# Attention and two feed-forward layers on one core: constant rows set once per buffer, zero rows and k's second copies moved by transfers, q loaded once for both chunks, h1 tiles stored in pairs

## The chip, the core and the metric

The kernel runs on one core of a Trainium2 chip. The metric is the device time of one execution in microseconds (us); the time before is the median of three runs. The engines are TensorE (PE, its weight loads shown apart as PEld), VectorE (DVE), ScalarE (ACT), GpSimd (POOL) and SyncE (SP), on whose queue almost all transfers (DMAs) are issued.

## What is computed

A decay attention over 4 batches, 8 heads, 576 rows and 64 columns a head, then two feed-forward layers on the 2304 x 512 result:

```python
scores = scale * np.matmul(q, k.transpose(0, 1, 3, 2))
cum = np.cumsum(np.log(np.clip(f, 0.0001, 1.0)), axis=-1)
decay = cum[:, :, :, None] - cum[:, :, None, :]
scores = np.where(causal, -1000000000.0, scores + decay)
attn = np.exp(scores - np.max(scores, axis=-1, keepdims=True))
attn = attn / (np.sum(attn, axis=-1, keepdims=True) + 1e-09)
x = np.matmul(attn, v)                 # then heads side by side: 2304 x 512
h = x @ w_in;   x = (h * (1.0 / (1.0 + np.exp(-1.702 * h)))) @ w_out
h = x @ w_in2;  out = (np.maximum(h, 0.0) + alpha * np.minimum(h, 0.0)) @ w_out2
```

All is fp32; a product is made from a rounded high part and a low remainder of each operand (fp32r), which is why casts and subtractions surround every matmul.

## The kernel before

Every operation is handed to a planner (`Plan.add`) with the engines that may run it, a duration for each, the buffers that it reads and writes, and a priority. `Plan.plan` (line 124) then places the operations one by one, each on the engine and at the time at which it could start, and so sets the order of the instructions on every engine and on SP's queue. At run time each engine works through its own list in order and waits on semaphores. A transfer is planned as 1500 ns, its bytes, and 750 ns (line 176), with 230 ns more (`LAT`) until a reader may start; SP is taken as busy for 610 ns an issue (line 198). Where PE would idle in the plan near the start, `run` (line 228) puts filler matmuls on `ident` (line 490) ahead of the operation.

The work has three parts. **Attention** runs until about 340 us. A unit is a pair of heads of a batch; its 576 query rows are two chunks, rows 0 to 255 and 256 to 575. Units 0 to 7 (batch 0) are `old` and get their transposed k and q from PE. Units 8 to 19 (batches 1 to 3) get them as follows. `load_qk` (line 723) loads a tile `raw` by four transfers, one for 32 partitions each, and DVE transposes it into `tk`. `stack` (line 742) makes two operands out of it for each head (`hh`): `KA` or `QA` (a cast, line 749), and `KB` or `QB`, which hold the low part (a subtraction, line 753) in one half of the partitions and a second copy of the high part in the other (line 756, a copy by ACT, DVE or POOL). `KA` and `QA` have constant rows besides: ones and zeros, set by memsets of `refill` (line 620) whenever a buffer is taken again, up to a limit given by its argument `first`, and in `QA` a row of zeros that is written anew for every chunk (line 806), since the row maxima later land in it (line 982 writes rows 0 to 2). `chunk` (line 895) computes scores for the row maxima (lines 925 and 927), masks them and takes the maxima on DVE (line 952), turns these (line 969) and writes them into `QA`. `chunk2` (line 1051) computes the scores again (line 1081, from `KA`, `KB`, `QA`, `QB`), takes the exponential (line 1097), and multiplies with v (lines 1016 and 1044). Operands are prepared `PRE = 2` steps ahead of the chunk that needs them.

**The first product** (`gemm1`, line 1159, matmuls of line 1180) is background work: once the rows of a block are done, its matmuls fill PE wherever a chunk's next operation is not yet ready. A result tile m (of 16 a block) is evacuated by ACT into `gg`, one of three buffers, and stored to `h1scr` (line 1186). **The rest** (lines 1203, 1424 and 1606) is matmul after matmul with streamed operands.

Of the kernel before, what the change touches and what calls it, by code (L numbers as in the profile page):

```python
# [7 lines left out]
F32 = mybir.dt.float32  # L8
# [77 lines left out]
class Plan:  # L86
# [37 lines left out]
    def plan(self, pen, hold_for, back):  # L124


        free = {}
# [24 lines left out]
        while avail:  # L152
# [42 lines left out]
            if eng == "PE":  # L195
                mode = o.mode
            if eng in QUEUE:
                free[QUEUE[eng]] = t + 610.0
                dma = end - 750.0
            else:  # L200
                free[eng] = end
                if port:
                    free["port"] = end
# [44 lines left out]
def kernel(  # L248
# [143 lines left out]

    ones = att.tile([P, 2, P], F32R, name="ones")
    p_z = sb("att", "Z", 2, [P, 2, P], F32R)
    p_raw = sb("att", "raw", 3, [P, S])
    p_tk = sb("att", "tk", 1, [P, S])

    p_ka = sb("att", "KA", 2, [P, 2, S], F32R)
# [130 lines left out]
    def a_move(n):  # L529
        return [*a_copy(n, HALF), ("POOL", c_pool(n), 0.0, True)]  # L530
# [189 lines left out]

    def load_qk(src, b, h0, w, c0, pri, actq):

        raw, T = Buf(p_raw), Buf(p_tk)
        for o in range(0, P, 32):
            hh, e_ = o // 64, o // 32 % 2
            d_ = DMA(32 * w * 4 * 1.6)
            if actq:
                d_.append(("ACTQ", d_[0][1], 300.0))  # L730
            plan.add(d_, lambda e, hh=hh, e_=e_, o=o: E[e].dma_start(
                raw.ap[o:o + 32, 0:w].rearrange("p (n d) -> p n d", d=32),
                src[b, h0 + hh, c0:c0 + w, 32 * e_:32 * e_ + 32].rearrange("(n p) d -> p n d", p=32),
            ), (), [(raw, o)], pri, QLAG if pri < QPRI else 0.0)
        plan.add([("DVE", 1.25 * w + 85.0)], lambda e: nc.vector.transpose(T.ap[:, :w], raw.ap[:, :w]), [raw], [T], pri)
        return T

    def split(T, w, hi, lo, pri):
# [3 lines left out]
    def stack(T, w, big, other, keys, swap, pri):  # L742

        half = [slice(64 * hh, 64 * hh + 64) for hh in range(2)]
        for hh, r in enumerate(half):
            plan.add(a_copy(w, HALF), lambda e, hh=hh, r=r: copy(e, big.ap[r, hh, :w], T.ap[r, :w]), [T], [(big, ("h", hh, k_)) for k_ in keys], pri)
        for hh, r in enumerate(half):  # L750
            x, y = (half[1 - hh], r) if swap else (r, half[1 - hh])
            rb = [(big, ("h", hh, k_)) for k_ in keys]
            plan.add([("POOL", c_pool(w), 0.0, True), ("DVE", c_half(w), BS, True)], lambda e, hh=hh, r=r, y=y: sub(
                e, other.ap[y, hh, :w], T.ap[r, :w], big.ap[r, hh, :w].bitcast(F32)
            ), [T, *rb], [(other, ("l", hh, k_)) for k_ in keys], pri)
            plan.add(a_move(w), lambda e, hh=hh, r=r, x=x: copy(e, other.ap[x, hh, :w], big.ap[r, hh, :w].bitcast(F32)), rb, [(other, ("h", hh, k_)) for k_ in keys], pri)

    RAW0 = {}

# [37 lines left out]
        plan.add([("ACT", c_act(w, True))], lambda e: copy(e, ov(hi), tv()), [T], [(hi, key)], pri)  # L797
        plan.add([("DVE", c_dve(w))], lambda e: sub(e, ov(lo), tv(), ov(hi).bitcast(F32)), [T, (hi, key)], [(lo, key)], pri)

    def prep_q(u, q0, q1, pri, actq, pet, old):  # L800
        b, h0, m = u["b"], 2 * u["hp"], q1 - q0
        first = u["first"]
        qa, qb = (Buf(p_q0), Buf(p_dq0)) if first else (Buf(p_qa), Buf(p_qb))
        if not old:
            refill(qa, OQ, 3 * m, lambda x: ((x[64:67, 0], 1.0), (x[0:64, 1], 0.0), (x[0:3, 1], 1.0)), pri - 1)
            plan.add([("POOL", 0.95 * m + 60.0)], lambda e: E[e].memset(qa.ap[0:1, 1, :m].bitcast(F32), 0.0), (), [(qa, ("d", 1))], pri)
            stack(load_qk(q, b, h0, m, q0, pri, actq), m, qa, qb, [0], True, pri)
            z = None
            if q0:
                z = Buf(p_z)  # L810
                refill(z, OLD - NP, 4 * P, lambda x: ((x, 0.0), (x[64:66, 0, 0:64], 1.0), (x[0:3, 1, 64:P], 1.0), (x[0:1, 1, 64:P], 0.0)), pri - 1)
                for hh in range(2):
                    r = slice(64 * hh, 64 * hh + 64)
                    plan.add(a_copy(64), lambda e, hh=hh, r=r: copy(
                        e, z.ap[r, hh, 64 * hh:64 * hh + 64], qa.ap[r, hh, m - 64:m].bitcast(F32)
                    ), [(qa, ("h", hh, 0))], [(z, hh)], pri)
            return dict(u, z=z, qa=qa, qb=qb)
# [14 lines left out]
        return dict(u, z=z, fdq=fdq, qa=qa, qb=qb, qh=qh, ql=ql, dq=dq)  # L832

    def prep(b, hp, n, pri, early, actq, plain, pet, old):
# [21 lines left out]
            if not first:  # L856
                rows()
        else:
            refill(ka, OLD, 3 * S, lambda x: ((x[64:67, 0], 1.0), (x[0:64, 1], 0.0), (x[0:3, 1], 1.0)), pri - 1)
# [299 lines left out]
    def gemm1(i, pri, vpri):  # L1159
# [13 lines left out]
        for m in range(NM):  # L1173
# [7 lines left out]

            for c0 in range(0, KT, 2):
                plan.add([("PE", 6 * c_mm(n))], lambda e, ph=ph, w=w, c0=c0: hmm(e, ph, w, c0), [(w, (0, 0)), (w, (0, 1)), xh[c0 // 2], xl[c0 // 2]], [ph], pri)
            g = Buf(p_gg)
            plan.add(a_out(n), lambda e, g=g, ph=ph: copy(e, g.ap[:, :n], ph.ap[:, :n]), [ph], [g], vpri)
            plan.add(DMA(P * n * 4), lambda e, g=g, m=m: nc.sync.dma_start(h1scr[:, m, t0:t0 + n], g.ap[:, :n]), [g], [(b_g1, (i, m))], vpri)

    done = {"i": 0}

# [155 lines left out]
    def operands(no, step):  # L1345
        b, hp, cs_ = seq[no]
        actq, pet, old = 2 <= no < ACTP, no < PET, no < OLD
        kv = prep(b, hp, CH[cs_[-1]][1], A0 + step - PRE, b == 0, actq, no < PLAIN, pet, old)
        return [prep_q(kv, *CH[c_], A0 + step + i - PRE, actq, pet, old) for i, c_ in enumerate(cs_)]

    units = {no: operands(no, no) for no in range(NP)}
    for i, (src, bsrc) in enumerate(((chi, b_ch), (cuml, b_cc))):
# [325 lines left out]
```

## Time and profile before

| what | us |
|---|---|
| median of three runs | 980.39 |
| the three runs | 978.27, 980.39, 980.99 |
| the profiled execution | 978.25 |
| its span | 976.5 |
| PE busy in the span | 958.9 (98%) |
| weight loads busy | 899.6 (92%) |
| DVE, ACT, POOL busy | 755.6, 629.3, 130.7 |

The profiled execution took 1.75 us beside its span, and 2.14 us less than the median. Matmuls are pipelined, so that the next one begins while the last is still shown as busy.

### The profile page before, as it was taken

What the parts mean: (1) busy time and instruction counts of PE and PEld (TensorE: products, weight loads), DVE (VectorE), ACT (ScalarE), POOL (GpSimd) and SP (SyncE); (2) the same over time, 40 slices, a digit from 0 to 9 for tenths busy, and PEclk for the clock granted to TensorE, in tenths of its full rate; (3) what the DMA queues carried; (4) which work ended last, traced back from release to release, by engine and by line L of the source; (5) the groups of instructions that cost most, each with busy time, mean ns of one, the idle gap of its engine ahead of it and who ended that gap; (6) DMA issues with size and microseconds to landing.
All of it is one profiled execution on the core that took longest, in us unless ns stands there. A gap on an engine that the chain in (4) does not pass through costs nothing.

```text
span 976.5 us, 18451 instructions
## 1 busy us (share of the span) xinstructions
PE 958.9 (98%) x6343; PEld 899.6 (92%) x6343; DVE 755.6 (77%) x1635; ACT 629.3 (64%) x1310; POOL 130.7 (13%) x273
## 2 busy tenths in 40 slices
PE   8999999999999999999999999999999999999998
PEld 6788899899999999988888988999999999999998
DVE  4889977788877699946558785788668967887876
ACT  6778986888777558867667795575555743333332
POOL 4236643222222102100000000000000000000000
PEclk9999999999999999999999999999999999999999
DMA  7866634444443136757888685778738495543523
GB/s 140 183 196 182 161 88 119 95 98 93 110 106 75 54 104 226 214 176 256 285 324 277 219 254 188 245 267 297 281 114 308 163 381 197 155 148 109 152 76 99
DMA packets 190015, 176.16 MB, mean 180 GB/s; under 512 B 106480, under 2 KB 164736, under 8 KB 187616
## 3 DMA queue, kind: packets, MB, share of 16 engines
q1 hardware_dynamic: 189904, 174.96, 58.1%
q8 instruction: 50, 0.82, 0.4%
q14 instruction: 45, 0.37, 0.1%
q10 hardware_dynamic: 16, 0.01, 0.0%
HBM read 110.95 MB, written 63.90 MB: 179 GB/s over the span
## 4 chain that ended last, share of the span: by engine, by line
PE 82%; DVE 7%; ACT 4%; DMA 3%; issue 2%; SPq 1%; POOL 1%; DVEq 0%; ACTq 0%; POOLq 0%
PE bk L1203 23%; PE bk L1424 20%; PE bk L1606 19%; PE bk L1180 8%; PE bk L1081 3%; PE bk L1016 2%; PE bk L1044 2%; DVE bk L952 1%; DMA u<-dscr 1%; PE bk L1086 1%; DVE el L524 1%; ACT e L1097 1%; PE bk L927 1%; DMA wraw<-in_moe_w_in_dram 1%; DVE KB L524 1%
## 5 line engine op out<-in xcount | busy, mean ns | idle before, releaser
L1203 PE MATMUL bk<-x,wS 128*128 128x384 f32 x912 | 160.4, 335 | 0.3 <-DVE lx L1229 0.2
L1203 PEld LDWEIGHTS bk<-x,wS 128*128 128x128 f32 x912 | 158.1, 188 | 1.2 <-DVE lx L1229 0.5
L1180 PE MATMUL bk<-xh,w 128*128 128x320 f32 (+2 forms) x640 | 156.6, 309 | 0.0
L1424 PE MATMUL bk<-lh,w 128*128 128x512 f32 (+1 forms) x640 | 146.9, 369 | 0.0
L1424 PEld LDWEIGHTS bk<-lh,w 128*128 128x128 f32 x640 | 112.9, 189 | 19.8
L1180 PEld LDWEIGHTS bk<-xh,w 128*128 128x128 f32 x640 | 111.3, 189 | 2.0 <-issue 1.4
L1180 PE MATMUL bk<-xl,w 128*128 128x320 f32 (+2 forms) x320 | 97.3, 304 | 0.1
L952 DVE CUSTOM_DVE_ANT_0 bk<-bk,mask 128x288 f32<-128x288 f32 (+4 forms) x160 | 74.9, 497 | 19.9 <-PE bk L927 17.1
L524 DVE TENSOR_TENSOR ll<-lx,lh 128x512 fp32r<-128x512 f32 (+1 forms) x80 | 50.9, 637 | 49.2 <-PE bk L1424 34.4
L519 ACT CAST x<-x 128x768 fp32r<-128x768 f32 (+3 forms) x57 | 47.3, 858 | 61.6 <-PE bk L1606 47.5
L1424 PE MATMUL bk<-ll,w 128*128 128x512 f32 (+1 forms) x320 | 81.2, 368 | 0.0
L1097 ACT ACTIVATE e<-bk 128x320 f32<-128x320 f32 (+4 forms) x224 | 63.2, 363 | 19.3 <-PE bk L1081 8.3
L1606 PE MATMUL bk<-wS,x 128*128 128x256 f32 x567 | 70.5, 284 | 0.0
L1606 PEld LDWEIGHTS bk<-wS,x 128*128 128x128 f32 x567 | 69.1, 192 | 0.0
L524 DVE TENSOR_TENSOR x<-x,x 128x768 fp32r<-128x768 f32 (+3 forms) x59 | 57.0, 983 | 15.4 <-ACT x L519 15.0
L1606 PE MATMUL bk<-wS,lh 128*128 128x256 f32 x378 | 68.7, 284 | 0.0
L1424 PEld LDWEIGHTS bk<-ll,w 128*128 128x128 f32 x320 | 57.1, 189 | 9.7
L519 ACT CAST lh<-x 128x768 fp32r<-128x768 f32 (+3 forms) x38 | 31.4, 851 | 53.7 <-PE bk L1606 48.4
L1390 ACT ACTIVATE lx<-lx 128x512 f32<-128x512 f32 (+1 forms) x80 | 46.8, 587 | 29.6 <-DVE ll L524 27.0
L1180 PEld LDWEIGHTS bk<-xl,w 128*128 128x128 f32 x320 | 60.5, 189 | 0.8 <-DVE xl L524 0.3
L1606 PEld LDWEIGHTS bk<-wS,lh 128*128 128x128 f32 x378 | 59.0, 192 | 0.0
L519 ACT COPY lx<-bk 128x384 f32<-128x384 f32 x72 | 34.2, 479 | 33.2 <-PE bk L1203 18.0
(230 smaller groups left out, 2153.8 us busy)
## 6 DMA issues: line engine op xcount, KB each, us to landing
h2scr<-lx SPq DMA_DIRECT2D x96, 192.0 KB
wraw<-in_moe_w_in_dram SPq DMA_DIRECT2D x32, 512.0 KB
wraw<-in_moe_w_out_dram SPq DMA_DIRECT2D x32, 512.0 KB
lx<-h1scr SPq DMA_DIRECT2D x64, 256.0 KB
x<-h2scr SPq DMA_DIRECT2D x32, 512.0 KB
w2scr<-wS SPq DMA_DIRECT2D x5, 1792.0 KB
tscr<-wS SPq DMA_DIRECT2D x4, 1792.0 KB
wS<-tscr SPq DMA_DIRECT2D x4, 1792.0 KB
```

The lines of the kernel that those rows point to most:

```text
L519: nc.scalar.copy(dst, src)
L524: E[e].tensor_tensor(dst, a, b, op=ALU.subtract)
L952: plan.add([("DVE", c_dve(c1 - c0))], lambda e, pm=pm, c0=c0, c1=c1, mk=mk, m0=m0, col=col, f0=f0: nc.vector.tensor_tensor_reduce(pm.ap[:, ...
L1016: nc.tensor.matmul(pb[hh].ap[:, c0:c1], vr.ap[:, t, hh, :], e32.ap[:, hh, e0:e0 + m], start=st, stop=sp, skip_group_check=True,)
L1044: nc.tensor.matmul(pb[hh].ap[:l.shape[1], s0 - q0:n], l, rhs.ap[:w, hh, :m], start=st, stop=sp, skip_group_check=True,)
L1081: nc.tensor.matmul(pss[hh].ap[:w, o_:o_ + m], x.ap[r, hh, a:a + w], y.ap[r, hh, s0 - q0:n], start=i == 0, stop=i == 1, skip_group_check=True)
L1097: plan.add([("ACT", c_act(x1 - x0, True))], lambda e, hh=hh, pss=pss, e32=e32, w=w, x0=x0, x1=x1: nc.scalar.activation(e32.ap[:w, hh, :x1 ...
L1180: nc.tensor.matmul(ph.ap[:, :n], w.ap[:, a, c, :], x[c // 2].ap[:, c % 2, :n], start=(c == 0 and j == 0), stop=(c == KT - 1 and j == 2))
L1203: nc.tensor.matmul(out.ap[:, :XH], wt(a, c), x.ap[:, b, c, :], start=(st and c == 0 and i == 0), stop=(c == 1 and i == 2), skip_group_chec ...
L1390: plan.add([("ACT", c_act(n))], lambda e: nc.scalar.activation(g.ap[:, :n], raw.ap[:, :n], AF.Gelu_apprx_sigmoid), [raw], [g], pri)
L1424: nc.tensor.matmul(py[d].ap[:, :n], w[:, a, d * P:(d + 1) * P], (lo if x else h).ap[:, :n], start=(k == 0 and (a, x) == (0, 0)), stop=(k = ...
L1606: nc.tensor.matmul(py[j].ap[:, t * HF:(t + 1) * HF], x.ap[:, q:q + P], w[:, o, a, :], start=(k == 0 and t == 0 and c == 0), stop=(k == NPA ...
```

## The change

Five things. (1) `refill` is given a smaller `first` for `QA` and `KA`, so that the constant rows are set once for each of the two buffers and no longer for the first six uses. (2) The zero row of `QA` comes from row 3 of the same tile, which stays zero, by a transfer. (3) k's second copies (`KB<-KA`) are transfers too. (4) q is loaded for all 576 rows at once by `load_raw`, and both chunks transpose their part of it; `raw` has two buffers, not three. (5) h1 tiles are evacuated into halves of a tile and stored two at a time; `gg` has two such tiles in place of three single ones. In the planner SP is taken as busy for 540 ns an issue in place of 610, which with the rest redraws the order on every engine.

```diff
-                free[QUEUE[eng]] = t + 610.0
+                free[QUEUE[eng]] = t + 540.0
...
-    p_gg = sb("p1", "gg", 3, [P, BW])
+    p_gg = sb("p1", "gg", 2, [P, 2, BW])
...
-    p_raw = sb("att", "raw", 3, [P, S])
+    p_raw = sb("att", "raw", 2, [P, S])
...
-    def load_qk(src, b, h0, w, c0, pri, actq):
+    def load_raw(src, b, h0, w, c0, pri, actq):
-        raw, T = Buf(p_raw), Buf(p_tk)
+        raw = Buf(p_raw)
...
+        return raw
+    def load_qk(src, b, h0, w, c0, pri, actq, raw=None, r0=0):
+        T = Buf(p_tk)
+        if raw is None:
+            raw = load_raw(src, b, h0, w, c0, pri, actq)
+        plan.add([("DVE", 1.25 * w + 85.0)], lambda e: nc.vector.transpose(T.ap[:, :w], raw.ap[:, r0:r0 + w]), [raw], [T], pri)
...
-            plan.add(a_move(w), lambda e, hh=hh, r=r, x=x: copy(e, other.ap[x, hh, :w], big.ap[r, hh, :w].bitcast(F32)), rb, ...
+            dup = DMA(64 * w * 4) if not swap else a_move(w)
+            plan.add(dup, lambda e, hh=hh, r=r, x=x: nc.sync.dma_start(
+                other.ap[x, hh, :w].bitcast(F32), big.ap[r, hh, :w].bitcast(F32)
+            ) if e == "SP" else copy(e, other.ap[x, hh, :w], big.ap[r, hh, :w].bitcast(F32)), rb, ...
...
-            refill(qa, OQ, 3 * m, ...
-            plan.add([("POOL", 0.95 * m + 60.0)], lambda e: E[e].memset(qa.ap[0:1, 1, :m].bitcast(F32), 0.0), (), [(qa, ("d", 1))], pri)
-            stack(load_qk(q, b, h0, m, q0, pri, actq), m, qa, qb, [0], True, pri)
+            refill(qa, OQ - NP, 3 * m, ...
+            plan.add(DMA(4 * m), lambda e: nc.sync.dma_start(qa.ap[0:1, 1, :m].bitcast(F32), qa.ap[3:4, 1, :m].bitcast(F32)), (), [(qa, ("d", 1))], pri)
+            stack(load_qk(q, b, h0, m, q0, pri, actq, raw, q0), m, qa, qb, [0], True, pri)
...
-            refill(ka, OLD, 3 * S, ...
+            refill(ka, OLD - NP, 3 * S, ...
...
-            g = Buf(p_gg)
+            if m % 2 == 0:
+                g = Buf(p_gg)
-            plan.add(DMA(P * n * 4), lambda e, g=g, m=m: nc.sync.dma_start(h1scr[:, m, t0:t0 + n], g.ap[:, :n]), [g], [(b_g1, (i, m))], vpri)
+            if m % 2:
+                plan.add(DMA(2 * P * n * 4), lambda e, g=g, m=m: nc.sync.dma_start(h1scr[:, m - 1:m + 1, t0:t0 + n], g.ap[:, :, :n]), [g], ...
...
+        raw = None if old else load_raw(q, b, 2 * hp, S, 0, A0 + step - PRE, actq)
```

In the lists of the engines the change takes away 12 fillers on PE (30 to 18), 19 instructions on ACT (1314 to 1295), 10 on DVE (1637 to 1627), 43 on POOL (278 to 235) and 40 issues on SP (826 to 786). No other matmul is added or taken away. Line numbers of the change lie 3 to 18 higher; the names carry buffer numbers.

PE at the end of batch 0's second chunks: the last scores for maxima of one unit, then the turning of the maxima (`ident_r,MX`). Before:

```order
L931 MATMUL bk_94<-KA_299,Z_107 128x288
L932 MATMUL bk_94<-KB_117,ones 128x288
L794 MATMUL bk_92<-ident,r_236 128x128 x2
L794 MATMUL bk_92<-ident,r_236 128x64
L490 MATMUL bk_87<-ident 128x128 x9
L969 MATMUL bk_87<-ident_r,MX_101 67x128 x2
```

And now:

```order
L944 MATMUL bk_94<-KA_284,Z_107 128x288
L945 MATMUL bk_94<-KB_117,ones 128x288
L490 MATMUL bk_90<-ident 128x128 x2
L1023 MATMUL bk_90<-e_102,r_106 64x256 x2
L1023 MATMUL bk_91<-e_102,r_106 64x256 x2
L1023 MATMUL bk_90<-e_111,r_106 64x128 x2
L1023 MATMUL bk_91<-e_111,r_106 64x128 x2
L982 MATMUL bk_93<-ident_r,MX_101 67x128 x2
```

Nine fillers became two, and eight matmuls with v (line 1010, now 1023), which stood ahead of these rows, stand between.

ACT around the preparation of k for one unit of batch 1 (`KA`, `KB`) and the evacuation of an earlier unit's result (`u`). Before:

```order
L519 CAST KA_299<-tk_595 64x576
L1136 COPY u_464<-bk_89 128x320
L1136 COPY u_464<-bk_94 128x320
L519 CAST KB_117<-KA_299 64x576 x2
L519 CAST VH_113<-VR_109 128x3x2x64
L1136 COPY u_382<-bk_90 128x256
```

And now:

```order
L519 CAST eh_1373<-e_112 128x2x256
L1149 COPY u_425<-bk_87 128x320
L1149 COPY u_425<-bk_91 128x320
L519 CAST VH_113<-VR_109 128x3x2x64
L519 CAST QA_435<-tk_581 64x256 x2
L519 CAST QB_118<-QA_435 64x256 x2
```

The two casts into `KB` are gone from between the copies.

POOL before, two chunks of batch 1 (`e` is the exponential being masked):

```order
L806 MEMSET QA_498 1x320
L998 AFFINE_SELECT e_111<-e_111 128x2x128
L524 TENSOR_TENSOR el_1427<-e_102,eh_1412 128x640
L806 MEMSET QA_406 1x256
L998 AFFINE_SELECT e_102<-e_102 128x2x128
```

SP's queue now, at a comparable place (`raw` are the loads of k and q, `cd<-u` and `dscr` the row sums of the chunk before):

```order
L819 DMA QA_495<-QA_495 1x16x20
L875 DMA KA_477<-cscr 2x576 x2
L888 DMA VR_110<-in_v_dram 64x2x64
L884 DMA VR_110<-in_v_dram 128x4x64 x2
L734 DMA raw_131<-in_k_dram 32x18x32
L1201 DMA h1scr<-gg_737 128x2x320
L767 DMA KB_119<-KA_477 64x576 x2
L734 DMA raw_131<-in_k_dram 32x18x32
L819 DMA QA_435<-QA_435 1x16x16
```

The zero rows and the copies into `KB` stand on SP among the loads and stores, and whatever is behind them there waits with them.

## Rows read from the trace of the kernel before

**Rows 1.** The page, part 1: busy us, share of the span, instructions.
```profile
PE 958.9 (98%) x6343; PEld 899.6 (92%) x6343; DVE 755.6 (77%) x1635; ACT 629.3 (64%) x1310; POOL 130.7 (13%) x273
```
**Rows 2.** Busy time by stretch: us, busy of each engine (count), PEclk, DMA share, GB/s.
```profile
50.00:100.00 50.00, 48.66 (x385) 41.50 (x384) 45.98 (x115) 40.31 (x98) 25.45 (x55) 1.00 0.62 180
100.00:150.00 50.00, 47.21 (x340) 45.07 (x339) 41.16 (x112) 42.42 (x106) 24.77 (x47) 1.00 0.52 128
150.00:200.00 50.00, 46.78 (x340) 44.75 (x339) 39.34 (x112) 39.67 (x101) 15.45 (x32) 1.00 0.44 102
200.00:250.00 50.00, 49.43 (x380) 48.13 (x379) 41.61 (x113) 41.10 (x107) 14.71 (x29) 1.00 0.44 99
250.00:300.00 50.00, 49.13 (x345) 46.89 (x345) 38.76 (x107) 38.75 (x102) 11.52 (x25) 1.00 0.45 103
300.00:350.00 50.00, 49.63 (x324) 48.39 (x323) 35.51 (x88) 29.26 (x74) 10.56 (x19) 1.00 0.22 65
...
700.00:800.00 100.00, 99.83 (x600) 99.51 (x600) 77.61 (x145) 57.91 (x114) 0.00 (x0) 1.00 0.64 229
```
**Rows 3.** Waits of PE, 50 to 350 us: us in total, times, longest.
```profile
PE bk L1044 <- ACT eh L519: 3.7, 4, 1.9
...
PE bk L1016 <- POOL e L998: 0.7, 1, 0.7
```
**Rows 4.** Waits of the weight loads, 50 to 350 us.
```profile
PEld bk L1044 <- ACT eh L519: 6.2, 10, 2.1
...
PEld bk L1081 <- ACT QA L980: 1.5, 4, 0.8
...
PEld bk L1016 <- POOL e L998: 1.2, 1, 1.2
```
**Rows 5.** Line 490, the fillers: duration ns min/median/max, first and last start.
```profile
L490 PE MATMUL bk<-ident x60: 218/276/582, 1.5 to 106.8; 128*128 128x128 f32 x54, 128*128 128x64 f32 x6
```
**Rows 6.** Timeline around the nine fillers: start us, us, engine, line, operation.
```profile
33.62 1.52 PE L1010 MATMUL bk<-e,r 128*64 128x256 f32 x16
...
36.23 2.27 PE L490 MATMUL bk<-ident 128*128 128x128 f32 x18
...
37.46 0.78 POOL L961 TENSOR_SCALAR MX<-MX 64x1 fp32r<-64x1 f32 x2 [0.51 <-DVE cd L1120]
...
38.26 0.36 PE L969 MATMUL bk<-ident_r,MX 128*67 128x128 f32 x2
```
**Rows 7.** Groups of instructions on ACT and POOL: count | busy us, mean ns | idle before.
```profile
L519 ACT CAST KB<-KA 64x576 fp32r<-64x576 f32 x22 | 14.8, 674 | 0.5
...
L623 POOL MEMSET KA<- 3x576 f32 (+1 forms) x18 | 10.7, 596 | 0.9
L806 POOL MEMSET QA<- 1x256 f32 (+1 forms) x24 | 8.3, 345 | 31.8 <-PE bk L1081 23.2 <-ACT u L1136 4.4 <-DVE el L524 2.2
```
**Rows 8.** Tiles raw, gg and KA: SP's issues, ns min/median/max each.
```profile
L731 SPq DMA_DIRECT2D raw<-in_q_dram x88: 312/451/1619, 85.5 to 301.0; - x88
...
L1186 SPq DMA_DIRECT2D h1scr<-gg x80: 319/350/703, 46.2 to 361.8; - x80
...
L862 SPq DMA_DIRECT2D KA<-cscr x24: 233/256/402, 79.1 to 295.7; - x24
```
**Rows 9.** Chain that ended last: transfers in it, start us, us to landing.
```profile
129.94 4.35 DMA u<-dscr
...
164.42 2.51 DMA cd<-u
```
**Rows 10.** Tile KB from 62 us on: first and last starts of its readers and copies.
```profile
L1081 PE MATMUL bk<-QB,KB x168: 193/309/464, 95.7 to 336.2; 128*128 128x320 f32 x72, 128*128 128x128 f32 x24, 128*128 128x256 f32 x24, 128*64 128x64 f32 x24
...
L519 ACT CAST KB<-KA x22: 668/673/693, 81.1 to 302.0; 64x576 fp32r<-64x576 f32 x22
```
**Rows 11.** Timeline: a zero row and the first matmul that reads it.
```profile
93.42 0.40 POOL L806 MEMSET QA<- 1x320 f32 x1
...
94.06 0.52 PE L927 MATMUL bk<-KA,QA 66*128 66x384 f32 x2
```

More of the change, by code (lines that the diff above doesn't have):

```diff
@@ L618, in filled @@
         return [fill[nm, len(p.bufs) - 1]] if len(p.bufs) <= p.n else []
+    refilled = []
     def refill(buf, first, n, sets, pri):
         if len(buf.pool.bufs) - first <= buf.pool.n:
+            refilled.append((buf, first))
             plan.add([("POOL", 0.95 * n + 120.0)], lambda e: [E[e].memset(x.bitcast(F32), y) for x, y in sets(buf.ap)], (), [buf], pri)
@@ L734, in load_qk @@
             ), (), [(raw, o)], pri, QLAG if pri < QPRI else 0.0)
-        plan.add([("DVE", 1.25 * w + 85.0)], lambda e: nc.vector.transpose(T.ap[:, :w], raw.ap[:, :w]), [raw], [T], pri)
+        return raw
[4 more added lines that the diff above has]
+        plan.add([("DVE", 1.25 * w + 85.0)], lambda e: nc.vector.transpose(T.ap[:, :w], raw.ap[:, r0:r0 + w]), [raw], [T], pri)
         return T
@@ L755, in stack @@
             ), [T, *rb], [(other, ("l", hh, k_)) for k_ in keys], pri)
-            plan.add(a_move(w), lambda e, hh=hh, r=r, x=x: copy(e, other.ap[x, hh, :w], big.ap[r, hh, :w].bitcast(F32)), rb, [(other, ("h", hh, k_)) for k_ in keys], pri)
+            dup = DMA(64 * w * 4) if not swap else a_move(w)
+            plan.add(dup, lambda e, hh=hh, r=r, x=x: nc.sync.dma_start(
+                other.ap[x, hh, :w].bitcast(F32), big.ap[r, hh, :w].bitcast(F32)
+            ) if e == "SP" else copy(e, other.ap[x, hh, :w], big.ap[r, hh, :w].bitcast(F32)), rb, [(other, ("h", hh, k_)) for k_ in keys], pri)
     RAW0 = {}
@@ L798, in load_pe, with prep_q @@
         plan.add([("DVE", c_dve(w))], lambda e: sub(e, ov(lo), tv(), ov(hi).bitcast(F32)), [T, (hi, key)], [(lo, key)], pri)
-    def prep_q(u, q0, q1, pri, actq, pet, old):
+    def prep_q(u, q0, q1, pri, actq, pet, old, raw=None):
         b, h0, m = u["b"], 2 * u["hp"], q1 - q0
@@ L804, in prep_q @@
         if not old:
-            refill(qa, OQ, 3 * m, lambda x: ((x[64:67, 0], 1.0), (x[0:64, 1], 0.0), (x[0:3, 1], 1.0)), pri - 1)
-            plan.add([("POOL", 0.95 * m + 60.0)], lambda e: E[e].memset(qa.ap[0:1, 1, :m].bitcast(F32), 0.0), (), [(qa, ("d", 1))], pri)
-            stack(load_qk(q, b, h0, m, q0, pri, actq), m, qa, qb, [0], True, pri)
+            refill(qa, OQ - NP, 3 * m, lambda x: ((x[64:67, 0], 1.0), (x[0:64, 1], 0.0), (x[0:3, 1], 1.0)), pri - 1)
+            plan.add(DMA(4 * m), lambda e: nc.sync.dma_start(qa.ap[0:1, 1, :m].bitcast(F32), qa.ap[3:4, 1, :m].bitcast(F32)), (), [(qa, ("d", 1))], pri)
+            stack(load_qk(q, b, h0, m, q0, pri, actq, raw, q0), m, qa, qb, [0], True, pri)
             z = None
@@ L858, in prep @@
         else:
-            refill(ka, OLD, 3 * S, lambda x: ((x[64:67, 0], 1.0), (x[0:64, 1], 0.0), (x[0:3, 1], 1.0)), pri - 1)
+            refill(ka, OLD - NP, 3 * S, lambda x: ((x[64:67, 0], 1.0), (x[0:64, 1], 0.0), (x[0:3, 1], 1.0)), pri - 1)
             stack(load_qk(k, b, h0, n, 0, pri, actq), n, ka, kb, range(len(ends)), False, pri)
@@ L1183, in gemm1 @@
                 plan.add([("PE", 6 * c_mm(n))], lambda e, ph=ph, w=w, c0=c0: hmm(e, ph, w, c0), [(w, (0, 0)), (w, (0, 1)), xh[c0 // 2], xl[c0 // 2]], [ph], pri)
-            g = Buf(p_gg)
-            plan.add(a_out(n), lambda e, g=g, ph=ph: copy(e, g.ap[:, :n], ph.ap[:, :n]), [ph], [g], vpri)
-            plan.add(DMA(P * n * 4), lambda e, g=g, m=m: nc.sync.dma_start(h1scr[:, m, t0:t0 + n], g.ap[:, :n]), [g], [(b_g1, (i, m))], vpri)
+            if m % 2 == 0:
+                g = Buf(p_gg)
+            plan.add(a_out(n), lambda e, g=g, ph=ph, m=m: copy(e, g.ap[:, m % 2, :n], ph.ap[:, :n]), [ph], [(g, m % 2)], vpri)
+            if m % 2:
+                plan.add(DMA(2 * P * n * 4), lambda e, g=g, m=m: nc.sync.dma_start(h1scr[:, m - 1:m + 1, t0:t0 + n], g.ap[:, :, :n]), [g], [(b_g1, (i, m - 1)), (b_g1, (i, m))], vpri)
     done = {"i": 0}
@@ L1348, in operands @@
         kv = prep(b, hp, CH[cs_[-1]][1], A0 + step - PRE, b == 0, actq, no < PLAIN, pet, old)
-        return [prep_q(kv, *CH[c_], A0 + step + i - PRE, actq, pet, old) for i, c_ in enumerate(cs_)]
+        raw = None if old else load_raw(q, b, 2 * hp, S, 0, A0 + step - PRE, actq)
+        return [prep_q(kv, *CH[c_], A0 + step + i - PRE, actq, pet, old, raw) for i, c_ in enumerate(cs_)]
     units = {no: operands(no, no) for no in range(NP)}
@@ L1642 @@
     est = plan.run(TRIES)
+    for p, first in {(x.pool, y) for x, y in refilled}:
+        assert {x.slot for x, _ in refilled if x.pool is p} == {x.slot for x in p.bufs[first:]}
     order.__exit__(None, None, None)
```

## The prediction

> **What bounds the kernel now.** I read the page's busy shares first. PE is busy for 98% of the span [rows 1]; no other engine comes near. So the time is PE's own work plus the moments in which PE stands still, and a change that adds and removes no product can only touch the second. Next I read the busy time by stretch, to see where PE stands still [rows 2]. From 700 us on it is busy for 99.83 of 100 us, so that nothing is to be had there. The attention stage is the loose one: from 50 to 350 us the six stretches sum to 290.84 us of 300, which leaves 9.16 us of idle PE. The clock granted is 1.00 of full speed in each, the higher of its two levels, so it plays no part.
>
> The same rows give a second measure. The weight loads are busy for 99.51 of 100 us from 700 us on, but for 274.73 of 300 us from 50 to 350, which leaves 25.27 us. Consecutive matmuls overlap, so a short stall can hide under a matmul that is still shown as busy; between 9.16 and 25.27 us lies what all stalls of the stage can be worth.
>
> Last I read who ends the waits. For PE, ACT's casts of the exponential come first with 3.7 us, and POOL's masking has 0.7 [rows 3]. For the weight loads ACT has 6.2 and 1.5 us in the two rows shown and POOL 1.2 [rows 4]. ACT is thus the engine that PE waits for most, and it is busy for 231.51 of the same 300 us [rows 2].
>
> **The change, part by part.** *Fillers.* The planner puts 18 in place of 30. The 30 leave 60 records [rows 5], two each; nine of them last 2.27 us [rows 6], 0.25 us each, so 12 fewer are 3.0 us of PE. But a filler stands where the plan sees a wait. The nine at 36.23 us cover a real one: POOL ends the maxima at 37.46 + 0.78 = 38.24, and PE goes on at 38.26 [rows 6]. Without other work PE would wait those 2 us all the same. The order of the change puts eight matmuls with v there, which took 1.52 us [rows 6] elsewhere before. So I take **-1.5 us**; the ends are 0 and -3.0.
>
> *k's second copies.* 22 casts of 674 ns, 14.8 us, leave ACT [rows 7], 6.4% of its 231.51 us; two more leave POOL. They stand between the evacuations and casts that PE waits for. PE's waits for ACT are 3.7 us by its own rows, 7.7 by the two rows of the weight loads [rows 3, 4]. A cast that comes earlier by one removed cast (0.67 us) is worth about a third of the longest wait of 2.1 us [rows 4], so I take a third of 7.7: **-2.5 us**. The ends are 0, since the planner knew of the casts and will pack ACT anew, and -7.7, all of these waits.
>
> The transfer that takes their place is slow, and hidden. The nearest row in its direction, SBUF to SBUF, landed in 2.51 us [rows 9]. The first copies start at 81.1 us and the first matmul that reads `KB` at 95.7 [rows 10]: 14.6 us of cover, against 1.35 for two casts. If the cover were gone, each of the 12 units would lose some 1.2 us. I cost it at nothing.
>
> *Constant rows.* 12 of 18 memsets of `KA` (596 ns) and 12 of 18 of `QA` go, and 24 of 345 ns for the zero rows [rows 7]: 12 x 0.596 + 24 x 0.345 = 15.4 us of POOL before those of `QA`. POOL is at half load at most [rows 2], and PE waits for it 0.7 us in one row, the weight loads 1.2 [rows 3, 4]. I take **-0.5 us**; the ends are 0 and -1.2.
>
> *Zero rows by transfer.* Each adds an issue on SP and some 2.2 us until it lands (2.51 less 0.345 of a memset). A zero row can be written only when the matmuls of two chunks earlier have read the tile: POOL waited 23.2 us for just that [rows 7]. Now SP does, with loads and stores queued behind it, and the matmul for the maxima, on PE, waits for the landing. The lead is short in places: one memset starts at 93.42 us and its reader at 94.06 [rows 11]. The planner counts 2.48 us for a transfer (1500 + 750 + 230 ns), close to the row of 2.51, and fills PE with background matmuls until then. I take **0**; the ends are 0 and +22 (below).
>
> *SP's queue.* 48 loads of q go, at 451 ns, and 40 stores of h1, at 350; 24 zero rows come, at 256 ns like the narrow `KA` rows [rows 8], and 24 copies, which I estimate at 0.5 us from the 451 ns of the loads. -21.6 - 14.0 + 6.1 + 12.0 = -17.5 us of issue time. Nothing on PE waits for SP by name, so it is worth 0; it is the reserve that the zero rows use up.
>
> *Two buffers of raw, pairs of h1.* With q held until its second chunk is transposed, k and q of a unit take both buffers, and the next k waits for one. What covers it is again the 14.6 us between k's copies and their first reader; a transpose that came a load's 2.5 us later would still fit. h1 is read back only when attention is over, so a store that waits for its pair costs 0; ACT could wait for `gg` a little more often, for which I add nothing.
>
> *The planner's 540 ns* adds no instruction. SP's medians of 256 to 451 ns [rows 8] lie under it, so the new plan is not too hopeful.
>
> The sum is -1.5 - 2.5 - 0.5 = **-4.5 us**. Against the profiled execution that is 978.25 - 4.5 = 973.75; the median of the runs shown lies 2.14 us above this execution, and against it the forecast is 980.39 - 4.5 = **975.9 us**. A measurement of this kernel can tell about 0.3% from no change: 2.9 us, so faster means under 977.4 and slower over 983.3.
>
> **The rivals.** *Stalls come back elsewhere (29%).* The planner places the whole stage anew, and its stalls are where its durations are wrong, not where an engine is full. For it: ACT is busy for 231.51 of 300 us, so it was not the limit. Against it: ACT ends most of PE's waits [rows 3, 4]. Then only the fillers' -1.5 is left: 978.9 us.
>
> *Zero rows land late (15%, the slower side).* The place is the matmul for the maxima of a second chunk. One transfer in the chain took 4.35 us to land [rows 9], 1.87 more than the planner's 2.48. If the twelve zero rows of second chunks land so, PE, which works in order, stands still for 12 x 1.87 = 22 us; if six do, 11.2. It decides as soon as more than two of them (4.5 / 1.87 = 2.4) are that late: then the gain is eaten. With six, 975.9 + 11.2 = 987.1 us. Against it: the transfer of 4.35 us spreads a row over 64 partitions (line 1146), a zero row is 1 to 1.3 KB in all. The Trainium skill, "SBUF — State Buffer", The DMA setup-cost knee, speaks against the change here: every transfer pays a roughly fixed 2 us whatever its size. The row of 2.51 us agrees with that.
>
> *All the waits go (12%).* If ACT's and POOL's lateness were the whole of what the weight loads show, -1.5 - 7.7 - 1.2 = -10.4 us: 970.0 us. For it: the weight loads' idle time, 25.27 us, is almost three times PE's 9.16 [rows 2]. Against it: a stall removed here can be filled only as far as the plan puts something else there. The Trainium skill, "Perfetto Trace Analysis", Identifying the Most-Contended Engine, would have this one: it says that matmul busy time is a poor measure of PE's headroom and weight-load busy time the better one. By the matmul rows the headroom of the stage is 9.16 us, by the skill's measure 25.27; my forecast lies inside both, and this rival only inside the second.
>
> **How the numbers follow.** The forecast has 44%. Its own range, 972 to 979, leaves it some six chances in 44 over 977.4. Faster: 38 + 12 + 5 of the rival at 978.9 (which may come out 1.5 us lower) = 55%. Same: 6 + 24 = 30%. Slower: 15%. For 8 in 10 the range takes the sum of the lower ends, -3.0 - 7.7 - 1.2 = -11.9: 968.5; and above it leaves out most of the late zero rows but keeps the edge of no change: 983.0.
>
> **What would show it.** Right: 36 matmul records on line 490; PE's idle time from 50 to 350 us down from 9.16 to 7 us or less and the weight loads' from 25.27 by 2 us or more; ACT's waits still first among PE's, but smaller; ACT's busy time there down by some 14 us; the first background matmul (line 1180) earlier by 1 to 2 us. After 400 us nothing differs but the start. Wrong: waits of PE or its weight loads for a transfer into `QA` or `KB`, over 4 us in all, would mean that the zero rows decide; an idle time as before with ACT's load lower would mean that the stalls come back.

## The result and the profile after

The change is slower: **987.84 us** (median of 5 runs, 984.33 to 990.88) against 980.05 us of the kernel before (5 runs, 978.27 to 980.99). The ratio is 1.0082, with a 95% interval of 1.0055 to 1.0110. The forecast was 975.9 us, with a range that ended at 983.0.

The profiled execution of the changed kernel took 990.88 us, its span 989.2. That is 12.7 us more than the span of 976.5 profiled before, so the profiles show more than the 7.8 us between the medians. The lines of the changed kernel are numbered 3 to 18 higher: 1044 became 1057, 1081 became 1094, 1146 became 1159, 1150 became 1163, 1180 became 1193.

First the busy shares, which answer to [rows 1]:

```profile
PE 962.3 (97%) x6319; PEld 901.6 (91%) x6319; DVE 756.0 (76%) x1625; ACT 616.2 (62%) x1291; POOL 115.5 (12%) x230
```

Then busy time by stretch in the same columns, which answers to [rows 2]:

```profile
50.00:100.00 50.00, 48.53 (x385) 41.40 (x384) 45.67 (x110) 39.34 (x95) 26.89 (x53) 1.00 0.62 176
200.00:250.00 50.00, 45.85 (x314) 43.85 (x314) 34.63 (x94) 33.73 (x91) 11.83 (x22) 0.90 0.48 102
50.00:350.00 300.00, 283.22 (x2013) 265.20 (x2012) 231.54 (x613) 213.35 (x555) 87.13 (x162) 0.98 0.49 119
700.00:800.00 100.00, 99.23 (x571) 98.59 (x570) 73.68 (x139) 58.31 (x118) 0.00 (x0) 1.00 0.63 223
```

Two things got worse in the attention stage. PE's idle time went from 9.16 to 300 - 283.22 = 16.78 us, and the weight loads' from 25.27 to 34.80. And the granted clock, 1.00 everywhere before, is 0.90 between 200 and 250 us. ACT, on the other hand, is busy for 213.35 us where it had 231.51.

The waits of PE from 50 to 350 us name the new releasers (us in total, times, longest); they answer to [rows 3]:

```profile
PE bk L1057 <- DVE el L524: 5.9, 8, 1.5
PE bk L982 <- POOL MX L974: 3.1, 3, 1.6
PE bk L982 <- DVE MX L965: 2.7, 4, 1.1
...
PE bk L1057 <- ACT eh L519: 0.4, 1, 0.4
```

ACT's casts, first before with 3.7 us, have 0.4. VectorE (DVE) is first now. The waits of VectorE itself in the same stretch show why. Before:

```profile
DVE xr L1150 <- DMA u<-dscr: 6.2, 7, 1.9
DVE cd L1142 <- DMA cd<-u: 0.2, 1, 0.2
```

After:

```profile
DVE xr L1163 <- DMA u<-dscr: 16.2, 14, 2.4
DVE cd L1155 <- DMA cd<-u: 3.6, 8, 0.8
```

These are the transfers of the row sums: the sums leave `u`, are inverted in `cd`, pass through `dscr` and come back spread out in `u`, where VectorE multiplies them into `xr`. VectorE works in order. While its `xr` waits for the transfer, the `el` of the next tile and the maxima stand behind it, and PE waits for those. The chain that ended last shows one such case, with `el`, in the changed kernel (start us, us, what):

```profile
194.98 3.83 DMA dscr<-cd
...
199.37 2.80 DMA u<-dscr
...
202.26 0.06 DVE xr L1163
...
202.60 0.83 DVE el L524
...
203.48 1.69 PE bk L1057 x6
```

In VectorE's timeline that `xr` has 1.83 us of idle time before it, and in PE's the matmuls at 203.48 have 1.49. What came next is in the stretches around it (columns as in [rows 2]):

```profile
200.00:202.50 2.50, 1.98 (x13) 1.49 (x12) 0.67 (x2) 2.21 (x5) 0.41 (x1) 1.00 0.31 65
202.50:205.00 2.50, 1.52 (x7) 1.48 (x8) 2.44 (x4) 1.39 (x4) 0.76 (x1) 0.77 0.68 139
205.00:207.50 2.50, 2.50 (x12) 2.36 (x12) 1.96 (x6) 1.00 (x3) 0.69 (x2) 0.55 0.81 157
...
232.50:235.00 2.50, 0.48 (x3) 0.20 (x3) 1.87 (x8) 0.37 (x1) 0.56 (x2) 0.91 0.11 10
235.00:237.50 2.50, 2.50 (x14) 2.50 (x15) 1.17 (x6) 0.43 (x1) 0.00 (x0) 0.50 0.72 154
```

As PE takes up work again after the stall, the clock goes to half (1.2 instead of 2.4 GHz). It happens again at 235 us, after PE had been busy for 0.48 us of 2.5 because the maxima came late. From the clock column, some 10 us of this profile ran at half clock; by my estimate about 5 us were lost by it. With the 7.62 us of added idle time that is 12.6 of the 12.7 us between the two spans. The near match is in part chance: over the whole span, PE's idle time grew by 9.3 us and its busy time by 3.4 (962.3 instead of 958.9), which already counts 3.4 us less of fillers.

Outside the stage little differs: PE stands idle there for 1.6 us more. The background matmuls of line 1180 ran from 42.4 to 360.9 us before:

```profile
L1180 PE MATMUL bk<-xh,w x640: 274/309/522, 42.4 to 360.9; 128*128 128x256 f32 x64, 128*128 128x320 f32 x64, 128*128 128x384 f32 x32
```

After, they begin 2.5 us earlier and end 10.9 us later:

```profile
L1193 PE MATMUL bk<-xh,w x640: 274/309/562, 39.9 to 371.8; 128*128 128x256 f32 x64, 128*128 128x320 f32 x64, 128*128 128x384 f32 x32
```

Last, SP's issues in the changed kernel, 50 to 350 us (duration ns min/median/max, first and last start), which answer to [rows 8]:

```profile
L819 SPq DMA_DIRECT2D QA<-QA x24: 529/550/726, 77.7 to 326.6; - x24
...
L767 SPq DMA_DIRECT2D KB<-KA x24: 477/538/595, 79.9 to 312.0; - x24
...
L1201 SPq DMA_DIRECT2D h1scr<-gg x34: 359/444/954, 55.5 to 343.5; - x34
```

And a dense piece of SP's timeline in the changed kernel, without a wait in it (start us, us, number of issues):

```profile
224.19 0.52 SPq L734 DMA_DIRECT2D raw<-in_k_dram  x1
224.80 0.65 SPq L819 DMA_DIRECT2D QA<-QA  x1
225.55 1.18 SPq L767 DMA_DIRECT2D KB<-KA  x2
226.82 1.20 SPq L1152 DMA_DIRECT2D cd<-u  x2
228.07 2.18 SPq L734 DMA_DIRECT2D raw<-in_k_dram  x3
230.35 0.45 SPq L1201 DMA_DIRECT2D h1scr<-gg  x1
```

From 224.19 to 230.35 us SP starts nine issues, one every 0.68 us, where the planner of the change counts 0.54. Over 62 to 345 us, the issues with less than 0.12 us between them follow each other every 0.57 us on average in the kernel before (304 of them, median 0.54) and every 0.60 us in the change (269, median 0.59).

**Theory A**: 540 ns is too short. The planner believes that SP is free earlier than it is, orders VectorE's row-sum steps too early, VectorE stands, PE stands behind it, and the clock falls. **Theory B**: the added transfers load SP and hold it up. **Theory J**, added later: every new figure draws a new order, and 540 was an unlucky draw.

### The profile page after: what moved, and what is told of

It is laid out like the page before. It is cut to its first block, busy times and chain, and to the rows that moved or that the text cites. A ratio compares the mean times of both kernels' runs of the same rounds, so it can differ in the third digit from the quotient of the medians.

```text
span 989.2 us, 18264 instructions
## 1 busy us (share of the span) xinstructions
PE 962.3 (97%) x6319; PEld 901.6 (91%) x6319; DVE 756.0 (76%) x1625; ACT 616.2 (62%) x1291; POOL 115.5 (12%) x230
## 4 chain that ended last, share of the span: by engine, by line
PE 79%; DVE 8%; DMA 6%; ACT 3%; issue 2%; SPq 1%; POOL 1%; DVEq 0%; ACTq 0%; POOLq 0%
PE bk L1218 21%; PE bk L1440 20%; PE bk L1622 18%; PE bk L1193 8%; PE bk L1094 3%; PE bk L1029 2%; DMA u<-dscr 2%; PE bk L1057 2%; DVE bk L965 1%; DMA dscr<-cd 1%; DVE el L524 1%; DMA h2scr<-lx 1%; PE bk L1099 1%; DVE QB L524 1%; PE bk L940 1%
## 5 line engine op out<-in xcount | busy, mean ns | idle before, releaser
L965 DVE CUSTOM_DVE_ANT_0 bk<-bk,mask 128x512 f32<-128x512 f32 (+4 forms) x160 | 74.6, 498 | 18.3 <-PE bk L940 16.7
L1110 ACT ACTIVATE e<-bk 128x320 f32<-128x320 f32 (+4 forms) x224 | 63.7, 359 | 18.2 <-PE bk L1094 8.3
L1011 POOL TENSOR_SCALAR_AFFINE_SELECT e<-e 128x256 f32<-128x256 f32 (+1 forms) x80 | 37.8, 483 | 158.3 <-ACT e L1110 133.1
```

Of the source, the lines that this page charges most:

```text
L965: plan.add([("DVE", c_dve(c1 - c0))], lambda e, pm=pm, c0=c0, c1=c1, mk=mk, m0=m0, col=col, f0=f0: nc.vector.tensor_tensor_reduce(pm.ap[:, ...
L1011: plan.add([("POOL", 150.0 + 0.82 * 2 * w, 0.0, True)], lambda e, e32=e32, w=w: nc.gpsimd.affine_select(e32.ap[:w, :, e0:e0 + w], e32.ap[: ...
L1110: plan.add([("ACT", c_act(x1 - x0, True))], lambda e, hh=hh, pss=pss, e32=e32, w=w, x0=x0, x1=x1: nc.scalar.activation(e32.ap[:w, hh, :x1 ...
```

## The experiments

**The planner's figure alone, both ways.** In the change 540 goes back to 610; in the kernel before 610 becomes 540:

```
-                free[QUEUE[eng]] = t + 540.0
+                free[QUEUE[eng]] = t + 610.0
```

The change with 610:

> The change with one number put back: the planner frees SP 610 ns after each issue, as in the kernel before, instead of 540. Theory A (540 is shorter than an issue of SP with the pause behind it, so VectorE's steps that need a transfer of the row-sum chain are ordered too early, VectorE stands, its el and its maxima come late, and TensorE with them): most of the loss goes, 973 to 982 us, PE's idle time over 50 to 350 us falls from 16.8 to 8 to 11 us, VectorE's wait for u<-dscr (16.2 us over 62 to 345) falls towards the 6.2 of before, and no stretch of the stage shows a granted clock under 0.97. Theory B (the added transfers themselves, zero rows and second copies, hold up SP): 985 to 990 us, with the waits of VectorE and PE as in the changed kernel.

The kernel before with 540:

> The kernel before with the planner's 540 ns in place of 610 and nothing else of the change; no instruction is added or removed, only the order moves. Theory A: slower than before, 983 to 990 us, with more waiting of VectorE for u<-dscr and cd<-u than 6.2 and 0.2 us, and of PE for VectorE's el. Theory B: 980 us as before, within 0.3%.

The change with 610 took 976.45 us (ratio to before 0.9977, 0.9962 to 0.9991); the kernel before with 540 took 988.49 us (1.0097, 1.0074 to 1.0119). The stage from 50 to 350 us, first of the change with 610:

```profile
50.00:350.00 300.00, 292.67 (x2114) 277.11 (x2114) 246.14 (x652) 219.36 (x565) 81.34 (x155) 1.00 0.50 124
```

Then of the kernel before with 540:

```profile
50.00:350.00 300.00, 284.40 (x2011) 266.07 (x2010) 241.28 (x643) 224.96 (x566) 105.13 (x208) 0.98 0.43 107
```

And the longest waits of PE in that stage of the kernel before with 540:

```profile
PE bk L1044 <- DVE el L524: 5.2, 8, 1.6
PE bk L1081 <- DVE QA L982: 3.9, 4, 1.5
```

One number, without any other part of the change, makes the whole loss: PE idle for 15.60 us, VectorE's `el` first among the waits, clock below 1.00. Without that number, the rest of the change has 7.33 us of idle time and full clock. Theory B would have left both kernels where they were.

**The two added transfers, at 540.** k's second copies go back to an engine, or q's zero row goes back to GpSimd:

```
-            dup = DMA(64 * w * 4) if not swap else a_move(w)
+            dup = a_move(w)
```
```
-            plan.add(DMA(4 * m), lambda e: nc.sync.dma_start(qa.ap[0:1, 1, :m].bitcast(F32), qa.ap[3:4, 1, :m].bitcast(F32)), ...
+            plan.add([("POOL", 0.95 * m + 60.0)], lambda e: E[e].memset(qa.ap[0:1, 1, :m].bitcast(F32), 0.0), ...
```

The copies on an engine:

> The change with k's second copies left where they were, on an engine (ScalarE where the planner finds it free) instead of a transfer: SP loses 24 issues of 0.525 us and 24 transfers, ScalarE gets 14.8 us back. Theory A: stays at 984 to 990 us, as the 540 stays. Theory B: 976 to 983 us, with VectorE's waits for u<-dscr near 6 us again.

The zero rows on GpSimd:

> The change with q's zero row set by GpSimd again, as before, instead of a transfer: SP loses 24 issues of 0.562 us, GpSimd gets 24 sets of some 345 ns. Theory A: 984 to 990 us. Theory B: 976 to 983 us. The recorded forecast's rival of late zero rows would also have 976 to 983 here, but PE and PEld waited only 0.4 us for these rows in the changed kernel, which speaks against it.

Measured: 982.94 us (1.0042, 1.0028 to 1.0057) and 988.31 us (1.0095, 1.0078 to 1.0112). The zero rows are cleared of the loss at 540. The copies gave 0.4% back by the ratios (1.0042 against 1.0082), about 3.9 us, between the two theories; the later runs show that this is within what a new order does by itself.

**More figures for the change.**

> The changed kernel with 575 in place of 540, about the spacing that SP's issues without a wait between them had in the trace (0.57 us before, 0.60 after, start to start). Theory A (a figure under the true spacing orders VectorE's steps too early, and the loss grows with the gap): between the two, nearer to 610's, 976 to 983 us. Theory J (any new order scatters by several us and 540 was an unlucky draw): no order between the values, anything from 974 to 990.

> The changed kernel with 640. Theory A: no further loss, 973 to 980 us, with VectorE's wait for u<-dscr no longer than the 8.2 us at 610. Theory J: anything from 974 to 990.

> The changed kernel with 545, the nearest neighbour of 540: the order is drawn anew but the error of the figure is the same. Theory A: 984 to 991 us, as with 540. Theory J: anything from 974 to 990.

575 gave 983.61 us (1.0046, 1.0029 to 1.0062), 640 gave 978.89 (0.9999, 0.9989 to 1.0010), 545 gave 985.30 (1.0065, 1.0050 to 1.0081). The order from 540 to 610 is theory A's, though 575 lies 0.6 us outside its range and 640 is 2.4 us above 610. 575 ns is SP's own mean spacing, and it is still 0.46% slower than the kernel before.

**The landing instead of the issue.** At 540, the planner takes each result 750 ns later:

```
-                        end = max(t + 1500.0, dma) + dur + 750.0
+                        end = max(t + 1500.0, dma) + dur + 1500.0
...
-                dma = end - 750.0
+                dma = end - 1500.0
```

> The changed kernel at 540, but the planner takes every transfer's landing as 750 ns later than it did (1.5 us instead of 0.75 us behind the data; issues and instructions are as in the change). Theory A in the form that VectorE stands because results are expected too soon, by whatever figure: VectorE's wait for u<-dscr falls below 10 us and the time to 976 to 983 us. If it is SP's issue rate alone that counts (queue order and not the landing), it stays at 984 to 991 us.

It took 982.17 us (1.0036, 1.0022 to 1.0050). VectorE's waits for the row-sum transfers almost vanish, and PE's idle time in the stage is 300 - 292.41 = 7.59 us, at full clock:

```profile
DVE cd L1155 <- DMA cd<-u: 2.1, 2, 1.2
DVE xr L1163 <- DMA u<-dscr: 1.4, 3, 0.7
```

So the link from a transfer expected too early to VectorE, and on to PE, is there: when the plan expects the results later, the stalls go, although SP's figure is still 540. But the time does not come down to that of 610. The cost has moved out of the stage: of the 6.2 us between this profiled span (980.2) and that of the change with 610 (974.0), PE's idle time before 50 us has 3.1 (6.54 instead of 3.47) and that from 350 to 400 us has 1.2 (1.73 instead of 0.51).

**The parts at 610, more caution, and a neighbour.** The edits are those above, each together with 610, and 620 alone.

> All of the change but the planner's figure (610) and k's second copies, which stay on an engine. It prices the transfer of the copies at a fair planner: the recorded forecast gave them 2.5 us of gain, so 979 us where the version with the copies by transfer had 976.5. If the copies' transfers cost as much as they free, 976.5 within 2 us; if they cost more, under 975.

> All of the change but the planner's figure (610) and q's zero rows, which GpSimd sets as before. The recorded forecast gave the zero rows by transfer nothing: 976.5 within 2 us. The recorded rival of late zero rows would have 972 to 974 here.

> The change with 610 and with landings planned 750 ns later as well, to see whether more caution gives more. If expecting results too early still costs something at 610 (VectorE waits 8.2 us for u<-dscr there): 971 to 975 us. If the issue figure had been the whole loss, 976.5 within 2 us, or slower, 978 to 982, where steps are now put off that could have started.

> The change with 620, a near neighbour of 610, for the scatter between new orders of the same quality. If the gain of 2.4 us over the kernel before at 610 belongs to the change and not to the draw: 975 to 978.5 us. If the scatter is as large as that: anything in 974 to 981.

Copies on an engine: 977.15 us (0.9984, 0.9975 to 0.9993). Zero rows on GpSimd: 981.54 (1.0026, 1.0015 to 1.0036), outside what I expected. Later landings: 982.88 (1.0050, 1.0032 to 1.0067), slower, and 0.9 us above the slower of my ranges, although VectorE waits for the row-sum transfers for only 1.4 us in all there. 620: 976.04 us (0.9969, 0.9957 to 0.9981). The copies by transfer and on an engine thus differ by 0.7 us, where the forecast had 2.5; and orders of the same figure differ by several us. The last runs show how far.

**The scatter of a new order.** The kernel before with 620, 640 and 550, and the change with 530:

> The kernel before with 620 in place of 610: a new order of the same quality. If the 2.4 to 3.0 us gained at 610 and 620 belong to the change's other parts: 978 to 983 us. If they are the draw: it may lie anywhere in 974 to 983.

> The kernel before with 640. The same alternatives as with 620: 978 to 983 us, or anywhere in 974 to 983; and not above 984 by either.

> The kernel before with 550. Theory A (a figure below SP's true spacing costs time, whatever the draw): 983 to 990 us, as its 988.5 at 540. Theory J (the draw): anywhere in 974 to 990, below 982 as likely as not.

> The changed kernel with 530. Theory A: 984 to 992 us. Theory J: anywhere in 974 to 990, below 982 as likely as not.

620 gave 975.80 us (0.9965, 0.9949 to 0.9981), 640 gave 988.09 (1.0080, 1.0056 to 1.0104), 550 gave 982.89 (1.0036, 1.0016 to 1.0055), the change with 530 gave 991.84 (1.0113, 1.0086 to 1.0139). 530 is theory A's and outside theory J's range; 550 lies 0.1 us under theory A's. The kernel before with 640 missed every expectation. Its PE is idle for only 6.01 us in the stage, but three rows of its stretches show what else went wrong:

```profile
107.50:110.00 2.50, 1.02 (x5) 0.44 (x3) 2.50 (x9) 2.23 (x5) 2.36 (x5) 1.00 0.69 143
110.00:112.50 2.50, 1.64 (x7) 1.22 (x8) 2.41 (x6) 1.24 (x2) 1.00 (x1) 0.64 0.35 57
112.50:115.00 2.50, 2.50 (x13) 2.50 (x13) 2.41 (x8) 0.75 (x2) 0.56 (x2) 0.50 0.10 16
```

Of the idle time 2.34 us fell into these first 5 us, in stalls of at most 0.85 us, and the clock went to half. With a second fall at 367 us, behind waits between the stages, some 14 us ran at half clock.

All orders with the planner's landing as it was, as ratios to the kernel before (PE's idle time is 300 us less its busy time from 50 to 350 us; the half-clock time is worked out from the clock of stretches of 2.5 us from 50 to 400):

| Figure | Kernel | Ratio | PE idle, us | Half clock, us |
|---|---|---|---|---|
| 530 | change | 1.0113 | 12.1 | 7 |
| 540 | change | 1.0082 | 16.8 | 10 |
| 540 | change, copies on an engine | 1.0042 | 13.3 | 10 |
| 540 | change, zero rows on GpSimd | 1.0095 | 14.6 | 7 |
| 540 | before | 1.0097 | 15.6 | 14 |
| 545 | change | 1.0065 | 12.6 | 10 |
| 550 | before | 1.0036 | 12.4 | 3 |
| 575 | change | 1.0046 | 11.4 | 0 |
| 610 | before | 1 | 9.2 | 0 |
| 610 | change | 0.9977 | 7.3 | 0 |
| 610 | change, copies on an engine | 0.9984 | 8.8 | 0 |
| 610 | change, zero rows on GpSimd | 1.0026 | 11.4 | 0 |
| 620 | change | 0.9969 | 8.4 | 3 |
| 620 | before | 0.9965 | 6.6 | 0 |
| 640 | change | 0.9999 | 9.0 | 0 |
| 640 | before | 1.0080 | 6.0 | 14 |

The eight orders under 600 average 1.0072 and the eight over 600 average 1.0000. The difference, 0.72% or 7.0 us, is about the size of the loss. Each of the eight short figures is slower than seven of the eight full ones. But single orders scatter by 0.3 to 0.4% (about 3 to 4 us) around the mean of their group, and by 0.8% once. The same comparison within one kernel comes out alike: four kernels were run with both 540 and 610 (the two kernels, and the change with the copies or the zero rows on an engine), and with 540 each is slower, by 0.58 to 1.05%, 0.82% on average.

The waits of theory A move the same way. VectorE's two waits for the row-sum transfers (`u<-dscr` and `cd<-u`, 50 to 350 us) add up to 9.5 to 21.2 us in the eight short orders, 14.8 on average, and to 4.6 to 12.2 us in the eight full ones, 8.8 on average; PE's waits for VectorE are 7.6 and 3.7 us on average. No single order can be read off them: the change with 620, among the fastest, has 12.2 us of these waits of VectorE. Nor do the table's two columns carry every order: with 530, PE stands idle outside the stage for 5.2 us more than in the kernel before. Theory A holds on average, and theory J has the size of the scatter right.

## Why the prediction was wrong

The step that failed is the one on the planner: "SP's medians of 256 to 451 ns [rows 8] lie under it, so the new plan is not too hopeful." It has three errors. The three rows were on the short side; another row of the same queue in the kernel before lay above 540 throughout:

```profile
L875 SPq DMA_DIRECT2D VR<-in_v_dram x13: 601/646/665, 64.1 to 297.4; - x13
```

This alone would not have changed the reading, since all 381 issues from 62 to 345 us last 0.485 us on average. But a duration is not a spacing: 0.05 to 0.1 us lie between issues, so SP started one every 0.57 us on average, between the planner's two figures. And whether a plan is too hopeful hangs on the landing too. The 4.35 us of `u<-dscr` [rows 9] was held against the planner's 2.48, but priced for the zero rows only. By its formula the plan counts some 2.5 us for `dscr<-cd` and 2.7 for `u<-dscr`; the chain of the changed kernel, which shows the ones that came last, has (start us, us to landing)

```profile
112.10 4.02 DMA dscr<-cd
116.69 4.53 DMA u<-dscr
...
175.93 3.39 DMA dscr<-cd
```

and 2.64 to 4.18 us for the other `u<-dscr`. So some landings were planned too short in both kernels, and the 70 ns taken off each issue came on top. The runs show that the lower figure costs time, not which of the two shortfalls, issue or landing, makes it cost.

I gave this edit no term, no end of the range and no rival. It was worth some 7 us on average, more than the whole sum. It is the one edit that "adds no instruction", and it moves every other one.

Point by point:

- *Fillers*: right in count (36 records on the filler line, as forecast), and the background matmuls start earlier, by 2.5 us (forecast 1 to 2). But most of the 24 records fewer went with the planner's figure: the kernel before with 540 has 38, the change with 610 has 54. What the fillers are worth by themselves was not tried.
- *k's second copies*: right that ACT's waits are what they relieve: PE's waits for the casts fell from 3.7 to 0.4 us, and ACT's load by 18.2 us (forecast 14; with 610, where the stage is not behind time, by 12.2). That this is worth 2.5 us is not shown: at 610 the version with the copies on an engine has ACT busy for 231.23 us instead of 219.36 and 2.2 us of PE's waits for the casts instead of 0.3, and takes 0.7 us more. At 540 the sign is the other way. The value is not to be told from zero in this scatter.
- *Zero rows by transfer*: right that they do not decide. They landed in 1.86, 1.97 and 2.08 us where the chain shows them, under the planner's 2.48 and far from the 4.35 of [rows 9]. The Trainium skill, "SBUF — State Buffer", The DMA setup-cost knee, has some 2 us for any transfer; these rows agree with that, and the 3.39 and 4.02 us of `dscr<-cd` above do not. In the changed kernel the weight loads waited 0.4 us for the zero rows in all. The rival named 987.1 us, nearly the result, by a mechanism that is not there. It is a real one in other orders, though: at 540 with the copies on an engine one zero row made PE wait for 1.6 us, and with 620 one made it wait for 2.33 us, and the clock fell behind it. That the version with GpSimd's zero rows is the slower one at 610 (1.0026 against 0.9977) was not foreseen and is not explained.
- *SP's queue*: mis-sized. A zero row's issue takes 0.550 us and not 0.256, a copy 0.538 (taken as 0.5), a paired store 0.444 instead of 0.350. Over the whole kernel the four forms of the sum (q loads, h1 stores, zero rows, copies) saved 12.4 us and not 17.5, and all other issues took 8.3 us longer, which leaves 4.1 (from 62 to 345 us: 184.7 to 180.1). Most of the reserve was not there.
- *The clock* "plays no part": true of the kernel before, not of what a few more stalls do to it. This was missing from the bounds: the sum of all stalls is not the most that stalls can cost.
- *Pairs of h1*: "I add nothing" for ACT and `gg`. PE waited once for that evacuation in the changed kernel, for 1.6 us; with 610 this wait is not there.
- *The rival of stalls that come back elsewhere* named the kind of cause, "its stalls are where its durations are wrong". But it let them only take back a gain, at 978.9 us, and not add to the idle time, and it did not point at the one duration that was edited.
- *The rival of all waits going*, 970.0 us: the best order found, the kernel before with 620, has 6.6 us of PE idle time and 20.9 of the weight loads, and takes 975.8 us. So at most 4.4 of the weight loads' 25.3 us of idle time went; no run shows the rest to be available. The Trainium skill, "Perfetto Trace Analysis", Identifying the Most-Contended Engine, prefers the weight loads' busy time as the measure of headroom; no run here comes near that headroom.
- *The sum without the planner's figure*: -4.5 us was forecast. At 610 the rest of the change gave 2.4 us (976.45 against 978.87 measured beside it). That the change's parts earn this is not shown: at 620 the two kernels are alike (0.9969 and 0.9965), and the averages over 540, 610, 620 and 640 differ by 0.3%, as much as one order scatters.

What stays open: the worth of the raw buffers, of the pairs of h1 and of the constant rows was not tried one by one, since each edit redraws the order and its scatter is larger than any of these terms. Why the best figure should lie a little above the mean spacing (610 or 620 against 0.57 to 0.60 us) and not at it (575) is not settled; the landings that were planned too short are one candidate. Later landings on top of 610 made it slower, so that more caution is not simply better. And the two late maxima at 233 to 235 us in the changed kernel stand behind a `cd` step of VectorE with 2.50 us of idle time for which the profile names no releaser; that it too waited for `cd<-u` was not shown.

No version is shown to beat both kernels by its own edits: the change with 610 is ahead by 0.23%, which is inside the scatter of orders. The fastest two, the change with 620 (976.04 us) and the kernel before with 620 (975.80 us), have the planner's figure in common.

## What to carry to other kernels

Where a planner sets the order, a constant of its model is an edit of every engine's queue: measure it as start-to-start spacing over all issues of that queue before it is lowered, and price it like a wait on the engine that works in order behind the transfer. The measured spacing need not be the best value: here 575 was slower than 610 and 620, so a few values on either side have to be run. Before a small gain is credited to an edit in such a kernel, draw a few orders that differ in nothing that matters; here those alone moved the time by 3 to 4 us, and once by 8. A releaser that vanishes from the list of waits is not yet time gained: look who comes first after it.

## What was not expected of the hardware

Some stalls cost more than they last. After PE had stood still for 1.49 us and again for 1.65 us in the changed kernel, for 2.33 us in the change with 620, and for three waits of 0.30, 0.69 and 0.80 us in the kernel before with 640, the granted clock went from 1.00 to 0.50 while PE was busy again. A background matmul of 256 columns then started every 0.21 us, where it had started every 0.12. The Trainium skill, "TensorE: Matmul & The Clock Gate", HAM oscillation — how this bites in real kernels, describes a kernel whose waits take the clock down so that the next products run slow. These traces agree in the order of events, a wait and then the fall.

But not every stall did it, and the length of one alone does not tell. The first of these lines, from the changed kernel, stands before a fall; the second, from the kernel before, and the third, from the change with 575, were followed by a clock of 1.00 (start us, us, instruction, idle time before it and who ended it):

```profile
203.48 0.62 PE L1057 MATMUL bk<-el,VH 128*128 128x320 f32 x2 [1.49 <-DVE el L524]
187.82 0.50 PE L1044 MATMUL bk<-eh,VH 128*128 128x256 f32 x2 [1.90 <-ACT eh L519]
247.21 0.50 PE L1057 MATMUL bk<-eh,VH 128*128 128x256 f32 x2 [2.32 <-ACT eh L519]
```

So part of the scatter between orders is whether a stall takes the clock down: the half-clock column above goes from 0 to 14 us, and the kernel before with 640 has the least idle time in the stage and one of the longest half-clock times.

SP's issues differ by form by a factor of two, and not by their bytes: 302 ns for the narrow rows of `KA` (4.5 KB) and 550 ns for a zero row (1 to 1.3 KB) in the changed kernel, and in the kernel before 506 ns for v's loads of 128 KB and 646 for those of 32 KB.
